# One head of a score pair: read from PSUM by ScalarE in place of a VectorE copy in SBUF

## The chip, the core and the metric

The kernel runs on one core of a Trainium2 chip. Its engines work side by side, each through its own list of instructions in order: TensorE (PE in the profile; its weight loads are listed as PEld) multiplies matrices and writes into PSUM, VectorE (DVE) and ScalarE (ACT) do elementwise work, GpSimd (POOL) some more of it, and SyncE (SP) issues DMAs. Engines wait for each other through semaphores. The metric is the device time of one execution in microseconds; the time before is the median of three runs.

## The reference

Two attention layers over 2048 positions with 32 heads of 18 dimensions, model width 576; their outputs stand side by side in `out`. Layer A is multi-query: 32 query heads share one key head and one value head, and every position attends to every other.

```
q = (x @ wq) as 32 heads;  k = x @ wk;  v = x @ wv          # A: one k, one v
p = softmax(q @ k^T * 18**-0.5);  out_A = concat(p @ v) @ wo
```

Layer B cuts the sequence into four segments of 512. In a segment each head does causal attention, and adds what a running memory of the earlier segments gives (a linear attention with its own denominator), weighed by a gate per head:

```
a_dot = softmax(q_s @ k_s^T * scale + mask) @ v_s
a_mem = phi(q_s) @ M / (phi(q_s) @ z + 1e-6)
o = g * a_mem + (1 - g) * a_dot;   M += phi(k_s)^T @ v_s;  z += sum phi(k_s)
```

Almost all of the elementwise work is the exponential of layer A's scores: 32 heads x 2048 x 2048.

## The kernel before

A first part (up to about 288 us of the span) projects x to queries, keys and values and stores them in DRAM. Then comes the attention, where the change lies, and at the end (from about 1363 us) the last output projections.

The attention works in **items**. For layer A an item is 128 keys (`kt`, 16 of them) by 512 queries (chunk `c`, 4) for a group of four heads (`hg`, 8); it is done as two **pairs** of heads (`pr` 0 and 1). So 32 blocks (`c`, `hg`) have 32 pairs each. Blocks of layer B (3 items each) are strewn between the first ones. Pairs are taken three to a **turn**: `turns[k]` lists them, and since 32 isn't a multiple of three, the last turn of a block has two. A block of layer A thus has eleven turns.

The loop over turns (L1177 to L1217) gives the engines their order, which is kept for TensorE, ScalarE and VectorE (`manual_schedule`). In turn `k` it does:

- `scores` (L935) for each of the turn's pairs: two matmuls (one a head, L950) into a PSUM tile `E` of 128 x 2 x 512, which takes two of the eight PSUM banks. There are three E buffers (`psE`, `bufs=3`); the other two banks are `O` and `F`. A tile's buffer can be used again when all that reads the tile is done.
- the exponentials, one ScalarE activation a pair over both heads (L968), in the order first, third, second pair (L1180).
- `run_fill`: a part of an output projection or of the memory's read-out (tile `F`, L801, L857).
- one third of the pending VectorE exponential, `slow` (L1192).
- `products` (L981): the matmuls of P with the values into `O` (L998), for the items of two turns before.
- `due`: stores, loads and weighing steps whose turn has come. Weighing (L785) runs on GpSimd, and each step is ordered behind `gate[-1]`, the last VectorE instruction noted. While `slow` holds work, `due` hands out no weighing step.

The **second pair** of each turn is `copied`: VectorE copies it from E into an SBUF tile `W` (L965), and ScalarE reads W. That lets go of E without waiting for ScalarE, which comes to this pair last.

In some turns of layer A (`BY_DVE`, L56: item 0 and item 9 for the second pair of heads, item 5 for the first, the third of these only in blocks in `third`) VectorE makes the exponential of one of the two heads itself. The positions are such that this is always the turn's second pair. There are 86 such turns: 10 blocks with two and 22 with three. `exponentials` (L920) reads E's first head with one `tensor_scalar` (L924) in the turn itself, and six more VectorE instructions (L926 to L931) follow in the second, third and fourth turn after. The other head's scores are copied to W (the half copy, 128 x 512, L965) and ScalarE makes their exponential (`hs = slice(1, 2)`) into the same tile PD.

Of the kernel before, what the change touches and what calls it, by code (L numbers as in the profile page):

```python
# [14 lines left out]
ALU = mybir.AluOpType  # L15
# [35 lines left out]
EXP_A = LOG2 * 2.0 ** 23  # L51
EXP_B = (127.0 + math.log2(0.00011720523372930181)) * 2.0 ** 23
# [23 lines left out]
def attention_pair_kernel(ctx, tc, a_xT, a_w, a_wo, b_xT, b_w, b_wo, b_beta, ident_d, hmask_d, bmask_d, cmask_d, sel_d, zmask_d, selx_d, sely_d, out):  # L76
    nc = tc.nc
# [79 lines left out]
    with ExitStack() as ph:  # L157
# [256 lines left out]
        for s in range(NSEG):  # L414
# [110 lines left out]
            if not last:  # L525
                e = p2.tile([128, 4, DH], F32, name="ph31")
# [101 lines left out]
    with tc.If(loose > 0, preferred_fallthrough_block=False):  # L628
        with ExitStack() as ph:
# [37 lines left out]
            with tc.For_i(0, H, 1) as h:  # L667
# [5 lines left out]
                for i in range(NKT):  # L673
                    s, j = divmod(i, 4)
                    n = 128 * (j + 1)
# [241 lines left out]
    slow, now, gate, third = [], [0], [], set()  # L917
    AFTER = mybir.DependencyInfo(mybir.DependencyClass.Sync, mybir.DependencyReason.SCHED_ONLY)

    def exponentials(p, e, whole):  # L920

        u, w = (pp.tile([128, 512], F32, name=nm, bufs=1) for nm in "nq")
        v, stt, y = nc.vector, nc.vector.scalar_tensor_tensor, p.bitcast(U32)
        v.tensor_scalar(y, e, EXP_A, EXP_B, op0=ALU.mult, op1=ALU.add)  # L924
        ops = [
            lambda: v.tensor_scalar(u.bitcast(U32), y, MANTISSA, ONE_BITS, op0=ALU.bitwise_and, op1=ALU.bitwise_or),  # L926
            lambda: v.tensor_scalar(w.bitcast(U32), y, EXPONENT, None, op0=ALU.bitwise_and),
            lambda: stt(p, u, POLY[0], u, op0=ALU.add, op1=ALU.mult),  # L928
            lambda: stt(p, p, POLY[1], u, op0=ALU.add, op1=ALU.mult),
            lambda: stt(p, p, POLY[2], p, op0=ALU.add, op1=ALU.mult),  # L930
            lambda: stt(p, p, POLY[3], w, op0=ALU.add, op1=ALU.mult),  # L931
        ]
        slow.extend((now[0] + 2 + i, p, ops[2 * i : 2 * i + 2], whole) for i in range(3))

    def scores(it, pr, copied):  # L935

        ab, c, hg, kt = it
        st = stacks[ab, c, hg // 2]
        h = 2 * (hg % 2) + pr
        e = psE.tile([128, 2, 512], F32, name="E")  # L940
        if ab == "A" and (kt, pr) == THIRD and not any(cost and k <= now[0] + 4 for k, cost, *_ in later):
            third.add((c, hg))
        dve = ab == "A" and (kt, pr) in by_dve(c, hg)
        p = pp.tile([128, 2, 512], F32, name="PD" if dve else "P", bufs=2 if dve else PBUFS)
        state[it, pr] = p
        n = 512 if ab == "A" else 512 - 128 * kt if kt < 2 else 384
        if ab == "A":
            for j, r0 in enumerate(HALF):
                rows = slice(r0, r0 + KR)
                nc.tensor.matmul(e[:, j], kstA[rows, 128 * kt : 128 * kt + 128], st[rows, h, :], start=True, stop=True)  # L950
            if dve:
                exponentials(p[:, 0], e[:, 0], p)
        else:
            for k, c0 in BKEYS[kt]:
                ks = slice(128 * k, 128 * k + 128)
                for j, r0 in enumerate(HALF):
                    rows = slice(r0, r0 + KR)
                    nc.tensor.matmul(  # L958
                        e[:, j, c0 : c0 + 512 - 128 * k], st[rows, 4 + h, ks], st[rows, h, 128 * k :], start=True, stop=True
                    )  # L960
        src, hs = e, slice(0, 2)
        if copied:
            src = pp.tile([128, 2, 512], F32, name="W", bufs=2)
            hs = slice(1, 2) if dve else slice(0, 2)
            gate.append(nc.vector.tensor_copy(src[:, hs, :n], e[:, hs, :n]))  # L965

        def exponential():
            nc.scalar.activation(p[:, hs, :n], src[:, hs, :n], AF.Exp, scale=SCALE)  # L968
            if ab == "B":

                m = len(BKEYS[kt])
                diag = p.rearrange("p a (b t) -> p a b t", t=256)[:, :, 0:m, 0:128]
                nc.gpsimd.affine_select(  # L973
                    diag, diag, pattern=[[0, 2], [0, m], [1, 128]], base=0, channel_multiplier=-1, compare_op=ALU.is_ge, fill=0.0
                )

        return exponential
# [36 lines left out]
    def by_dve(c, hg):  # L1014

        return [x for n, x in enumerate(BY_DVE) if n < 2 or (c, hg) in third]
# [112 lines left out]
    with tc.manual_schedule(engines={ENG.PE, ENG.Activation, ENG.DVE}):  # L1129
# [47 lines left out]
        for k in range(len(turns) + 2):  # L1177
            now[0] = k
            exps = [scores(its[n], pr, i == 1) for i, (n, pr) in enumerate(turns[k])] if k < len(turns) else []
            for i in (0, 2, 1) if len(exps) == 3 else range(len(exps)):  # L1180
                exps[i]()
# [167 lines left out]
```

## Time and profile before

| | |
|---|---|
| time, median of 3 runs | 1409.04 us (1406.99 to 1409.36) |
| span of the profiled execution, first to last instruction | 1404.7 us |
| TensorE matmuls busy | 1383.6 us, 98% |
| ScalarE busy | 1199.5 us, 85% |
| VectorE busy | 1047.3 us, 75% |
| GpSimd busy | 233.3 us, 17% |
| mean granted TensorE clock | 0.997 |

The page gives the profiled execution no time of its own beside the span; the span lies 4.3 us below the median of the runs. In the views a row has the start in us, the duration, the engine, the line, the operation, out<-in, shapes and a count; several instructions in a row of the same kind are merged into one row. Activations overlap: the next begins before the one ahead has written its last result, so that what an activation costs ScalarE is the distance from its start to the next start, and what a reader waits for is its end. Ends of matmuls are modelled. An idle time in brackets is followed by what ended it.

### The profile page before, as it was taken

What the parts mean: (1) busy time and instruction counts of PE and PEld (TensorE: products, weight loads), DVE (VectorE), ACT (ScalarE), POOL (GpSimd) and SP (SyncE); (2) the same over time, 40 slices, a digit from 0 to 9 for tenths busy, and PEclk for the clock granted to TensorE, in tenths of its full rate; (3) what the DMA queues carried; (4) which work ended last, traced back from release to release, by engine and by line L of the source; (5) the groups of instructions that cost most, each with busy time, mean ns of one, the idle gap of its engine ahead of it and who ended that gap; (6) DMA issues with size and microseconds to landing.
All of it is one profiled execution on the core that took longest, in us unless ns stands there. A gap on an engine that the chain in (4) does not pass through costs nothing.

```text
span 1404.7 us, 41217 instructions
## 1 busy us (share of the span) xinstructions
PE 1383.6 (98%) x17452; PEld 837.7 (60%) x17452; DVE 1047.3 (75%) x1563; ACT 1199.5 (85%) x1481; POOL 233.3 (17%) x335
## 2 busy tenths in 40 slices
PE   9999999989999999999999999999999999999998
PEld 6787888745554555555555555555555555555558
DVE  6656456467787778787878878777879778887884
ACT  4543434479999999999999999999999999999991
POOL 2441000003302310412110122113010220001002
PEclk9999999999999999999999999999999999999999
DMA  9766546567575345332322452233103321120023
GB/s 283 259 213 188 168 147 216 183 175 219 151 200 180 120 139 181 95 120 85 112 59 71 133 158 60 94 104 93 51 27 94 115 75 40 31 72 21 17 68 124
DMA packets 91284, 173.63 MB, mean 124 GB/s; under 512 B 14702, under 2 KB 23015, under 8 KB 90668
## 3 DMA queue, kind: packets, MB, share of 16 engines
q1 hardware_dynamic: 84680, 160.93, 36.9%
q0 software_dynamic: 1664, 4.78, 1.3%
q10 hardware_dynamic: 4752, 5.24, 1.2%
q8 instruction: 138, 2.26, 0.7%
q14 instruction: 50, 0.41, 0.1%
HBM read 99.65 MB, written 70.67 MB: 121 GB/s over the span
## 4 chain that ended last, share of the span: by engine, by line
PE 64%; ACT 6%; DVE 4%; issue 2%; DMA 1%; POOL 0%; SPq 0%; POOLq 0%; DVEq 0%; ACTq 0%
PE O L998 31%; PE E L950 19%; PE F L801 11%; ACT P L968 6%; PE E L958 3%; DVE W L965 2%; PE F L857 1%; DMA o<-oA 0%; DVE sm L750 0%; DVE PD L930 0%; DVE PD L928 0%; POOL o L785 0%; DMA rb<-rA 0%; DMA o<-o 0%; DVE o L862 0%
## 5 line engine op out<-in xcount | busy, mean ns | idle before, releaser
L968 ACT ACTIVATE P<-E 128x1024 f32<-128x1024 f32 (+1 forms) x800 | 787.6, 1076 | 4.4 <-PE E L950 4.2
L965 DVE COPY W<-E 128x1024 f32<-128x1024 f32 (+2 forms) x416 | 453.3, 1090 | 145.2 <-PE E L950 83.9
L998 PE MATMUL O<-P,VA 128*32 128x256 f32 x7504 | 507.6, 380 | 0.0
L968 ACT ACTIVATE P<-W 128x1024 f32<-128x1024 f32 (+1 forms) x330 | 369.9, 1121 | 6.1 <-DVE W L965 5.6
L998 PEld LDWEIGHTS O<-P,VA 128*32 128x32 f32 x7504 | 259.8, 110 | 138.0 <-issue 6.1
L950 PE MATMUL E<-stA,kstA 56*128 56x512 f32 x1920 | 317.0, 430 | 2.0 <-ACT P L968 1.8
L950 PEld LDWEIGHTS E<-stA,kstA 56*128 56x128 f32 x1920 | 155.3, 184 | 158.3 <-issue 94.2
L973 POOL TENSOR_SCALAR_AFFINE_SELECT P<-P 128x256 f32<-128x256 f32 (+1 forms) x192 | 94.6, 493 | 414.7 <-ACT P L968 376.7
L785 POOL TENSOR_TENSOR o<-o,rb 126x512 f32<-126x512 f32 (+1 forms) x55 | 72.8, 1348 | 431.1 <-DVE PD L931 185.1
L801 PE MATMUL F<-woB,o 126*32 126x192 f32 (+1 forms) x1920 | 126.6, 338 | 0.0
L998 PE MATMUL O<-PD,VA 128*32 128x256 f32 x688 | 88.9, 379 | 0.0
L801 PEld LDWEIGHTS F<-woB,o 126*32 126x32 f32 (+1 forms) x1920 | 38.7, 108 | 74.9 <-issue 69.6
L998 PE MATMUL O<-P,vseg 128*32 128x256 f32 (+2 forms) x1536 | 81.4, 344 | 0.1
L924 DVE TENSOR_SCALAR PD<-E 128x512 uint32<-128x512 f32 x86 | 59.2, 689 | 23.5 <-PE E L950 21.7
L1007 DVE COPY oe<-O 128x512 f32<-128x512 f32 x64 | 44.3, 692 | 42.4 <-PE O L998 39.8
L253 PE MATMUL pj<-xh,wBh 128*126 128x512 f32 x180 | 72.2, 401 | 0.0
L253 PE MATMUL pj<-xh,wBl 128*126 128x512 f32 x180 | 71.7, 398 | 0.0
L122 ACT CAST qp<-pj 126x512 fp32r<-126x512 f32 (+1 forms) x54 | 31.0, 584 | 44.2 <-DVE kmB L459 27.8
L123 DVE TENSOR_TENSOR qp<-pj,qp 126x512 fp32r<-126x512 f32 (+1 forms) x54 | 36.8, 686 | 37.8 <-ACT qp L122 37.8
L801 PE MATMUL F<-woA,o 126*32 126x192 f32 (+1 forms) x960 | 64.0, 338 | 0.0
L958 PE MATMUL E<-stB 56*128 56x256 f32 (+3 forms) x512 | 61.6, 348 | 2.1 <-ACT P L968 1.3
L998 PEld LDWEIGHTS O<-P,vseg 128*32 128x32 f32 x1536 | 49.0, 110 | 24.3 <-issue 1.9
(206 smaller groups left out, 1573.2 us busy)
## 6 DMA issues: line engine op xcount, KB each, us to landing
stB<-kB SPq DMA_DIRECT2D x96, 144.0 KB
stB<-qB SPq DMA_DIRECT2D x32, 288.0 KB
stA<-qA SPq DMA_DIRECT2D x30, 288.0 KB
oA<-oe SPq DMA_DIRECT2D x32, 256.0 KB
oB<-oe SPq DMA_DIRECT2D x32, 256.0 KB
qA<-qp SPq DMA_DIRECT2D x16, 504.0 KB
kB<-qp SPq DMA_DIRECT2D x16, 504.0 KB
qB<-qp SPq DMA_DIRECT2D x16, 504.0 KB
```

The lines of the kernel that those rows point to most:

```text
L123: hold(nc.vector.tensor_tensor(qp[:R, 1, :n], src, qp[:R, 0, :n].bitcast(F32), op=ALU.subtract))
L253: nc.tensor.matmul(dst, w[:, c0 : c0 + M], x, start=i == 0, stop=i == len(ops) - 1)
L785: ins = tc.keep_in_program_order(nc.gpsimd.tensor_tensor(dst, a, b, op=op))
L801: nc.tensor.matmul(dst[32 * j : 32 * j + 32], parts[ab, c][: RT[t], t, r0 : r0 + 32], wo[ab][: RT[t], t, c0 : c0 + n], start=start, stop=stop,
L924: v.tensor_scalar(y, e, EXP_A, EXP_B, op0=ALU.mult, op1=ALU.add)
L950: nc.tensor.matmul(e[:, j], kstA[rows, 128 * kt : 128 * kt + 128], st[rows, h, :], start=True, stop=True)
L958: nc.tensor.matmul(e[:, j, c0 : c0 + 512 - 128 * k], st[rows, 4 + h, ks], st[rows, h, 128 * k :], start=True, stop=True)
L965: gate.append(nc.vector.tensor_copy(src[:, hs, :n], e[:, hs, :n]))
L968: nc.scalar.activation(p[:, hs, :n], src[:, hs, :n], AF.Exp, scale=SCALE)
L973: nc.gpsimd.affine_select(diag, diag, pattern=[[0, 2], [0, m], [1, 128]], base=0, channel_multiplier=-1, compare_op=ALU.is_ge, fill=0.0)
L998: nc.tensor.matmul(o[32 * j : 32 * j + 32, q0 : q0 + n], v, p[:, j % 2, p0 : p0 + n], start=m == hf == 0, stop=last and hf == 1,)
L1007: nc.vector.tensor_copy(osb, o)
```

## The change

In `scores`, a pair of which VectorE makes one head is not copied any more: `src` stays E and only the other head (`slice(1, 2)`) goes through the activation, out of PSUM. The other second pairs are copied as before. So that the list `gate` still has an entry for such a turn, the `tensor_scalar` at the head of `exponentials` is put into it.

```diff
@@ def exponentials
-        v.tensor_scalar(y, e, EXP_A, EXP_B, op0=ALU.mult, op1=ALU.add)
+        gate.append(v.tensor_scalar(y, e, EXP_A, EXP_B, op0=ALU.mult, op1=ALU.add))
@@ def scores
-        src, hs = e, slice(0, 2)
-        if copied:
+        src, hs = e, slice(1, 2) if dve else slice(0, 2)
+        if copied and not dve:
             src = pp.tile([128, 2, 512], F32, name="W", bufs=2)
-            hs = slice(1, 2) if dve else slice(0, 2)
-            gate.append(nc.vector.tensor_copy(src[:, hs, :n], e[:, hs, :n]))
+            gate.append(nc.vector.tensor_copy(src[..., :n], e[..., :n]))
```

## The prediction

> **What bounds the kernel now.** I read the page's busy times first, then the busy times of the attention part alone, then the waits, then the order of time inside one block. The views agree that two engines are full at once.
>
> ```profile
> PE 1383.6 (98%) x17452; PEld 837.7 (60%) x17452; DVE 1047.3 (75%) x1563; ACT 1199.5 (85%) x1481; POOL 233.3 (17%) x335
> ...
> 288.00:1362.00 1074.00, 1066.72 (x15244) 576.17 (x15248) 862.97 (x1204) 1064.30 (x1215) 177.07 (x261) 1.00 0.33 101
> ...
> ACT P L968 <- DVE W L965: 5.6, 13, 0.8
> ACT P L968 <- PE E L950: 4.2, 5, 2.0
> ACT PD L968 <- DVE W L965: 0.5, 1, 0.5
> ...
> by line: PE O L998 47.5%; PE E L950 34.7%; PE F L801 18.4%
> ```
>
> The second line is the stretch from 288 to 1362 us: TensorE is busy 1066.7 of 1074 us and ScalarE 1064.3; the columns after them show VectorE at 863 and GpSimd at 177. ScalarE waits 10.3 us in all. The last line is the chain of waits over 1160 to 1185 us: there it never leaves TensorE. So the stage is paced by TensorE and ScalarE in turn, with about 10 us of room on either; VectorE has 20% free.
>
> How one turn runs is seen in a block of eleven turns late in the kernel, of which the first, fourth and seventh are changed turns (those with a half activation PD). First ScalarE, from the half activation of the first changed turn on, then TensorE's six score matmuls of the turns behind:
>
> ```profile
> 1165.36 0.63 ACT L968 ACTIVATE PD<-W 128x512 f32<-128x512 f32 x1
> 1165.89 1.94 ACT L968 ACTIVATE P<-E 128x1024 f32<-128x1024 f32 x2
> 1167.69 1.08 ACT L968 ACTIVATE P<-W 128x1024 f32<-128x1024 f32 x1
> 1168.64 1.96 ACT L968 ACTIVATE P<-E 128x1024 f32<-128x1024 f32 x2
> ...
> 1171.40 1.97 ACT L968 ACTIVATE P<-E 128x1024 f32<-128x1024 f32 x2
> 1173.20 0.69 ACT L968 ACTIVATE PD<-W 128x512 f32<-128x512 f32 x1
> 1173.72 1.99 ACT L968 ACTIVATE P<-E 128x1024 f32<-128x1024 f32 x2
> ...
> 1181.04 0.74 ACT L968 ACTIVATE PD<-W 128x512 f32<-128x512 f32 x1
> 1181.63 1.97 ACT L968 ACTIVATE P<-E 128x1024 f32<-128x1024 f32 x2
> ...
> 1184.40 1.06 ACT L968 ACTIVATE P<-E 128x1024 f32<-128x1024 f32 x1
> ```
>
> ```profile
> 1165.14 0.96 PE L950 MATMUL E<-stA,kstA 56*128 56x512 f32 x6
> 1167.79 0.96 PE L950 MATMUL E<-stA,kstA 56*128 56x512 f32 x6
> 1170.43 0.97 PE L950 MATMUL E<-stA,kstA 56*128 56x512 f32 x6
> 1173.10 0.95 PE L950 MATMUL E<-stA,kstA 56*128 56x512 f32 x6
> ...
> 1181.03 0.96 PE L950 MATMUL E<-stA,kstA 56*128 56x512 f32 x6
> 1183.68 0.96 PE L950 MATMUL E<-stA,kstA 56*128 56x512 f32 x6
> ```
>
> TensorE needs 2.65 us a turn (1167.79 to 1170.43). ScalarE needs 2.75 in a plain turn (1165.89 to 1168.64: two activations of 0.90 and one out of W of 0.95) and 2.32 in a changed one (1171.40 to 1173.72: the PD activation holds it 0.52 only). Three turns with one changed cost ScalarE 7.82 and TensorE 7.95: a tie, which is why a wait moved onto either is hardly covered.
>
> **The change part by part.**
>
> ```profile
> L965 DVE COPY W<-E 128x512 f32<-128x512 f32 x86 | 58.5, 681 | 0.0
> L968 ACT ACTIVATE PD<-W 128x512 f32<-128x512 f32 x86 | 61.6, 716 | 0.5 <-DVE W L965 0.5
> ```
>
> *Removed: 86 copies of half a pair.* VectorE loses 58.5 us of its 863. It is not on the path; what can be won is ScalarE's waits for a copy, 5.6 + 0.5 us, and only those that fall within a turn or two of a changed turn, since a copy removed shortens VectorE's queue by about 0.6 us there and nowhere else. Bounds: 0 and 6.1. I take 1.5.
>
> *Moved: the operand of 86 activations from SBUF to PSUM.* No row has a 128x512 activation out of E. The nearest are the full ones: from one start to the next, 0.90 out of E (1171.40 to 1173.20 is two) and 0.95 out of W (1167.69 to 1168.64). If the difference is per instruction, the half one falls from 0.52 to 0.475: 86 x 0.045 = 3.9 us of ScalarE time; if it is per element, half that; if the half form shows none, 0. I take 0.045, and carry it in the walk below.
>
> *Added: E is kept longer.* There are three E buffers for three pairs a turn. The copy gave the second pair's buffer back early; ScalarE takes the pairs in the order first, third, second, so now that buffer comes free with the last activation of the turn. What TensorE does when a copy is late is shown by one turn of before:
>
> ```profile
> 527.39 2.01 ACT L968 ACTIVATE P<-E 128x1024 f32<-128x1024 f32 x2
> 528.10 0.67 DVE L965 COPY W<-E 128x512 f32<-128x512 f32 x1
> 529.09 0.19 PEld L950 LDWEIGHTS E<-stA,kstA 56*128 56x128 f32 x2 [0.41 <-issue]
> 529.09 1.11 PE L950 MATMUL E<-stA,kstA 56*128 56x512 f32 x6
> 529.46 0.30 PEld L950 LDWEIGHTS E<-stA,kstA 56*128 56x128 f32 x4 [0.18 <-ACT P L968]
> ...
> L950 PE MATMUL E<-stA,kstA x1920: 382/393/503, 384.2 to 1360.7; 56*128 56x512 f32 x192
> ```
>
> The copy had ended at 528.77, yet the second pair (529.46) waited for ScalarE's second activation (end 529.40): the buffers are handed on in the order in which they were expected free. I therefore let the next turn's second pair take the third pair's buffer, and its *third* pair the one now kept by the PD activation. Also from these rows: 0.06 us from the end of an activation to the weight load, and a scores row of 1.11 instead of 0.96 for a pair that started 0.03 late, so a stalled pair costs 0.11 more to refill the pipeline. The third pair is due 0.57 after the first (0.96 less the median 0.39). Queued behind the waiting matmul are the turn's F and O matmuls and the next turn's scores; ScalarE waits for those. How soon it does:
>
> ```profile
> 475.52 0.95 PE L950 MATMUL E<-stA,kstA 56*128 56x512 f32 x6
> 476.06 1.94 ACT L968 ACTIVATE P<-E 128x1024 f32<-128x1024 f32 x2
> ```
>
> This is a turn in which ScalarE stood ready; an activation begins 0.54 after its pair's first matmul.
>
> Now the walk through the block. *First changed turn.* The PD activation ends at 1165.36 + 0.63 - 0.04 = 1165.95; the third pair may start at 1166.01 instead of 1165.14 + 0.57 = 1165.71: 0.30 + 0.11 = **0.41 us late**, and everything on TensorE behind it. The next scores start at 1167.79 + 0.41 = 1168.20, ScalarE can begin at 1168.74, but is ready at 1168.64 - 0.05 = 1168.59: it is now 0.10 behind the old trace. *Second.* PD starts at 1173.30 and ends at 1173.95; the third pair, due at 1173.10 + 0.41 + 0.57 = 1174.08, no longer waits (1174.01). But ScalarE, ready at 1173.30 + 0.475 = 1173.78, waits for the scores begun at 1173.51: until 1174.05, now 0.33 behind. *Third.* PD from 1181.37 to 1182.07; the third pair, due at 1182.01, starts at 1182.13: 0.12 + 0.11, TensorE 0.64 behind. ScalarE starts the next turn at 1181.44 + 0.54 = 1181.98 (0.35 behind) and the one after at 1183.68 + 0.64 + 0.54 = 1184.86 (0.46 behind).
>
> So such a block loses 0.46 us by ScalarE's count and 0.64 by TensorE's, and the plain turns that follow, at 2.65 and 2.75, give neither back. I take 0.50 for three changed turns, 0.167 each: 86 x 0.167 = 14.4 us, with the 0.045 already in it. Less the 1.5 of copy waits, **about +13 us**; I add 1 for blocks where the half activation is longer than here (its mean is 0.716, in this block 0.63 to 0.74): **+14**.
>
> *Moved: the entry in `gate`* from the copy to the tensor_scalar ahead of it. GpSimd's weighing is not handed out while the list `slow` holds work, and it does from the changed turn on, so the entry used is a later one: 0. Without that cover a GpSimd step would start 0.6 us earlier, with GpSimd 17% busy. No DMA is issued, removed or moved past another on SP's or GpSimd's queue. The W tile is taken 86 times less; only copies wait for it.
>
> **The rivals.**
>
> *A, TensorE has room and takes the wait in.* Then only the savings stay: 3.9 us of activations and up to 6.1 of copy waits, -4 to -10, say 1403. It decides at 0.4 us of slack a changed turn. For it: ScalarE is as full as TensorE, and where the turn holds less TensorE work the stall is free. Against it: the turn is 2.65 with or without a wait, and the chain between 1160 and 1185 is TensorE alone. The Trainium skill speaks for A: its page "Perfetto Trace Analysis", section "Identifying the Most-Contended Engine", says that matmul busy time is no good measure of how full TensorE is and that the weight loads' share should be used. By that rule the 576 of 1074 us of weight loads would leave nearly half free, and the result would be A's; I hold the chain against it, since the matmuls of a turn follow each other without a gap.
>
> *B, stall and savings cancel.* The first pair of turns loses 0.10 only; if the refill of 0.11 isn't paid and VectorE's shorter queue ends most copy waits, the sum is within 2.8 us of zero: 1409.
>
> *C, the buffers are handed on in the fixed order*, so that the next turn's second pair waits for the last activation. It is due some 0.28 earlier than the third, so each changed turn loses about 0.2 us more: +14 + 17 = +31, 1440. Against it: the row at 529.46.
>
> That the change doesn't do what it says would show as PD<-W rows; I give it nothing, the edit being two lines.
>
> **How the numbers follow.** The profiled execution's span is 1404.7 us; +14 makes 1418.7. The median of the runs, 1409.04, is 4.3 above the span, so I predict 1409 + 14 = 1423 us. Chances: forecast 0.58 (its own range 1413 to 1432), C 0.12, B 0.16, A 0.14. The range that holds 8 in 10 reaches from the upper part of A to C: 1404 to 1440. A measurement of this kernel can tell 0.2% (2.8 us) from no change: faster 0.14, same 0.16, slower 0.70.
>
> **What the changed profile would show.** 86 rows PD<-E in place of PD<-W, near 0.68 us each, held 0.475 from start to start; 330 copies in place of 416. In the turn after a changed one, score weight loads that wait for ScalarE's PD activation, for the third pair (if for the second, C holds). ScalarE's waits for TensorE's scores, now 4.2 us, grow to 15 or more: that is the loss itself. If they stay under 6 us, A or B is right. Waits of ScalarE on W near 6 us mean that nothing was won on VectorE. The forecast is wrong if a changed turn is followed by scores on time, or if TensorE's turn shrinks below 2.65.

## The result and the profile after

| | before | after |
|---|---|---|
| time, median (lowest to highest of the runs taken together) | 1409.2 us (1406.99 to 1409.36) | 1421.44 us (1420.54 to 1422.1) |
| span of the profiled execution | 1404.7 us | 1418.4 us |
| mean granted TensorE clock | 0.997 | 0.995 |

The changed kernel takes 1.0093 times as long, with an interval of 1.0078 to 1.0107: 12.2 us more by the medians, 13.7 by the spans. The granted clock differs by 0.002, which would be worth 3 us at the most (0.002 of 1409, an estimate), so at least three quarters of the time were lost in the order of the work.

The busy times of the page after, and the busy times of the attention alone (engine by engine in the order PE, PEld, DVE, ACT, POOL):

```profile
PE 1397.3 (99%) x17452; PEld 837.9 (59%) x17452; DVE 1002.7 (71%) x1477; ACT 1205.1 (85%) x1481; POOL 234.2 (17%) x335
...
288.00:1376.00 1088.00, 1080.61 (x15250) 577.23 (x15251) 818.43 (x1118) 1070.41 (x1215) 177.60 (x261) 1.00 0.33 100
```

VectorE has 44.6 us less to do over the span and 86 instructions fewer. From the first score matmul to the last turn of the attention it is 14.4 us more than before, so all of the loss lies there (the stretch shown is 14 us longer than the one of before, 288 to 1362), and TensorE counts as busy in nearly all of it again. That share can't show the stall, since the rows of a stalled turn (below) have it inside the busy time of the score matmuls. The waits show it.

What TensorE's weight loads wait for, in the attention part of before and then of after (us in total, times, longest). A weight load is the first instruction of a score matmul, so it carries the wait for a free E:

```profile
PEld E L950 <- issue: 99.8, 245, 1.9
PEld E L950 <- ACT P L968: 59.3, 159, 1.1
```

```profile
PEld E L950 <- ACT P L967: 101.4, 259, 1.4
PEld E L950 <- issue: 52.3, 131, 1.4
PEld E L950 <- ACT PD L967: 22.8, 81, 0.7
```

The last row is new: 81 of the 86 half activations are now what a score load waited for, and each of these 81 loads is that of a third pair. The other two rows say less than they seem to. Most of both is the bracket that every turn's first load has anyway, 0.41 us whether it is put down to issue or to ScalarE (1174.54 below, and 0.41 again at 1177.62, there under ScalarE's name); between the traces it has mostly changed its name.

The operations of the changed lines after (columns: busy us, mean ns of one, idle ahead of it):

```profile
L967 ACT ACTIVATE P<-E 128x1024 f32<-128x1024 f32 x704 | 694.8, 1047 | 10.9 <-PE E L950 5.4
L964 DVE COPY W<-E 128x1024 f32<-128x1024 f32 x298 | 364.5, 1223 | 164.8 <-PE E L950 128.9 <-ACT P L967 24.0 <-PE E L958 8.5
...
L967 ACT ACTIVATE PD<-E 128x512 f32<-128x512 f32 x86 | 54.3, 631 | 0.3 <-DVE PD L924 0.3
...
L964 DVE COPY W<-E 128x768 f32<-128x768 f32 x32 | 30.6, 958 | 32.9 <-PE E L958 31.0 <-ACT P L967 1.9
```

All 86 half activations read E, and 298 + 32 = 330 copies are left: the change does what it says.

Now the block of turns at the place of the one in the prediction, first on ScalarE, then TensorE's matmuls with the score weight loads of the middle turn (start, duration):

```profile
1174.77 0.60 ACT L967 ACTIVATE PD<-E 128x512 f32<-128x512 f32 x1
1175.25 1.95 ACT L967 ACTIVATE P<-E 128x1024 f32<-128x1024 f32 x2
1177.06 1.09 ACT L967 ACTIVATE P<-W 128x1024 f32<-128x1024 f32 x1
1178.22 1.94 ACT L967 ACTIVATE P<-E 128x1024 f32<-128x1024 f32 x2
```

```profile
1172.32 0.96 PE L950 MATMUL E<-stA,kstA 56*128 56x512 f32 x6
...
1174.54 1.39 PE L950 MATMUL E<-stA,kstA 56*128 56x512 f32 x6
1175.86 0.53 PE L801 MATMUL F<-woA,o 126*32 126x192 f32 x8
...
1177.62 0.96 PE L950 MATMUL E<-stA,kstA 56*128 56x512 f32 x6
1178.51 0.53 PE L801 MATMUL F<-woA,o 126*32 126x192 f32 x8
```

```profile
1174.54 0.19 PEld L950 LDWEIGHTS E<-stA,kstA 56*128 56x128 f32 x2 [0.41 <-issue]
1174.93 0.19 PEld L950 LDWEIGHTS E<-stA,kstA 56*128 56x128 f32 x2 [0.21 <-ACT P L967]
1175.42 0.19 PEld L950 LDWEIGHTS E<-stA,kstA 56*128 56x128 f32 x2 [0.30 <-ACT PD L967]
```

The half activation runs from 1174.77 to 1175.37, and 0.05 us later the third pair's weights are loaded, at 0.88 after the turn's first matmul. In a turn without a wait all six follow each other (the row at 1172.32: 0.96 for the six). The scores take 1.39 instead of 0.96, the F matmuls begin at 1.32 instead of 0.89, and the next scores come 3.08 us after this turn's (1177.62 less 1174.54) where the turn took 2.65 before. ScalarE begins the third of its activations at 1177.06, could begin the next at 1177.06 + 0.95 = 1178.01, and begins it at 1178.22, 0.60 after the scores.

Over all 32 blocks, in the turn after a changed one, by the place of the changed turn in its block (from the starts of the score matmuls in the two traces, all 86 turns; means for the third pair's start after the turn's first matmul, medians for the turn's length; the last column counts the turns that are over 0.2 us longer than the same turn of before):

| changed turn of the block | third pair, before | after | turn's length, before | after | over 0.2 us longer |
|---|---|---|---|---|---|
| first | 0.64 us | 0.91 us | 2.65 us | 3.08 us | 22 of 32 |
| second | 0.59 | 0.67 | 2.65 | 2.73 | 10 of 32 |
| third | 0.59 | 0.62 | 2.65 | 2.77 | 1 of 22 |

These are 33 long turns in 32 blocks: one in each of 31 blocks, two in one. A block has one stall, mostly behind its first changed turn. In nine of the ten blocks where the first is spared, all of which follow a block of layer B, its half activation has ended about 0.5 us after the next turn's first matmul, before the third pair is due at 0.57; there the second has the stall. Behind a stall ScalarE runs less far behind TensorE: in the second changed turn its first activation began 0.99 us after the turn's first score matmul before and 0.73 after (medians), and its half activation ended 0.87 us after the next turn's first matmul before and 0.49 after. So the third pair then finds its buffer nearly free when it is due.

### The profile page after: what moved, and what is told of

It reads as the page before. It is cut to its first block, busy times and chain, and to the rows that moved or that the text cites. A ratio compares the mean times of both kernels' runs of the same rounds, so it can differ in the third digit from the quotient of the medians.

```text
span 1418.4 us, 41046 instructions
## 1 busy us (share of the span) xinstructions
PE 1397.3 (99%) x17452; PEld 837.9 (59%) x17452; DVE 1002.7 (71%) x1477; ACT 1205.1 (85%) x1481; POOL 234.2 (17%) x335
## 3 DMA queue, kind: packets, MB, share of 16 engines
q1 hardware_dynamic: 84680, 160.93, 36.4%
## 4 chain that ended last, share of the span: by engine, by line
PE 70%; ACT 4%; DVE 3%; issue 2%; DMA 1%; SPq 0%; POOLq 0%; DVEq 0%; ACTq 0%
PE O L997 33%; PE E L950 21%; PE F L801 11%; ACT P L967 4%; PE E L958 3%; DVE W L964 1%; PE F L857 1%; DVE P L1142 1%; DMA rb<-rA 0%; DMA o<-o 0%; DVE sm L750 0%; DVE PD L928 0%; DVE PD L930 0%; DVE P L1161 0%; SPq L812 0%
## 5 line engine op out<-in xcount | busy, mean ns | idle before, releaser
L967 ACT ACTIVATE P<-E 128x1024 f32<-128x1024 f32 (+1 forms) x800 | 767.2, 1025 | 10.9 <-PE E L950 5.4
L964 DVE COPY W<-E 128x1024 f32<-128x1024 f32 (+1 forms) x330 | 395.1, 1197 | 197.7 <-PE E L950 128.9
L967 ACT ACTIVATE P<-W 128x1024 f32<-128x1024 f32 (+1 forms) x330 | 353.7, 1072 | 8.5 <-DVE W L964 8.4
L950 PE MATMUL E<-stA,kstA 56*128 56x512 f32 x1920 | 330.5, 438 | 2.8 <-ACT P L967 2.3
```

Source lines behind the costliest of these rows:

```text
L964: gate.append(nc.vector.tensor_copy(src[..., :n], e[..., :n]))
```

## The experiments

For each, the ratio is that to the kernel before, on the same chip. Differences in us are ratios times 1407.

**The entry in `gate` alone.** The kernel before, with only the one line of `exponentials` changed.

```diff
-        v.tensor_scalar(y, e, EXP_A, EXP_B, op0=ALU.mult, op1=ALU.add)
+        gate.append(v.tensor_scalar(y, e, EXP_A, EXP_B, op0=ALU.mult, op1=ALU.add))
```

> The kernel before, with nothing of the change but the entry in `gate` for the tensor_scalar of a changed turn (the half copy is made and noted as well). My theory (the cost is the E buffer kept until ScalarE has read it): no difference, 1409 within 3 us. Rival (the order given to GpSimd's weighing steps takes part in the loss): slower, up to the changed kernel's 1421.

Measured: 1406.63 us, ratio 1.0002 (0.9992 to 1.0011). This part of the change costs nothing, as the prediction priced it.

**The late release without VectorE's relief.** The changed kernel, in which VectorE still makes the 86 half copies, into a W that nobody reads.

```diff
             gate.append(nc.vector.tensor_copy(src[..., :n], e[..., :n]))
+        elif copied:
+            spare = pp.tile([128, 2, 512], F32, name="W", bufs=2)
+            nc.vector.tensor_copy(spare[:, hs, :n], e[:, hs, :n])
```

> The changed kernel, but VectorE makes the 86 half copies all the same, into a W tile that nobody reads; ScalarE reads E. The buffer is kept as long as in the changed kernel, VectorE has its old load. Theory: the changed kernel's time or a little over it, 1421 to 1425, since VectorE's relief was worth 1.5 us. Rival (VectorE's relief is worth much and hides a larger loss): over 1427. Rival (the time went into something that the missing copy changes on VectorE, not into the buffer): back to 1409.

Measured: 1422.52 us, 1.0115 (1.0098 to 1.0132). VectorE's work is that of before here, and only who frees E, and from where ScalarE reads, has changed; the loss is there in full. So it comes from that and not from what VectorE does next. The 44.6 us that VectorE gains are worth 3 us by the ratios (1.0115 against 1.0093) and 1 by the medians, and the intervals overlap: little, and not told from nothing.

**Only the first, or only the second changed turn of each block.** The changed kernel, with the half copy kept in all but the 32 turns of item 0 (in the other run of item 5, `(5, 0)` in the condition). The `tensor_scalar` is not put into `gate` in these two runs.

```diff
-        if copied and not dve:
+        if copied and not (dve and (kt, pr) == (0, 1)):
...
-            gate.append(nc.vector.tensor_copy(src[..., :n], e[..., :n]))
+            gate.append(nc.vector.tensor_copy(src[:, hs, :n], e[:, hs, :n]))
```

> The change in the first changed turn of each block alone (32 of the 86); the others copy as before. Theory (what counts is how late ScalarE runs behind TensorE, and a stall leaves less for the next): one such turn a block costs nearly as much as all three, 0.3 us a block: 1417 to 1420. Rival (each changed turn costs the same 12.2/86 = 0.14 us): 1409 + 4.5 = 1413.7.

> The change in the second changed turn of each block alone (32 of the 86). Theory: there ScalarE runs 0.9 to 1.1 us behind TensorE instead of 0.65, so that the third pair is late by itself although the walk of the prediction gave this turn no stall after a stalled first one: 0.3 us a block, 1418 to 1421. Rival (additive): 1413.7. First and second alone together then cost more than the whole change.

Measured: 1415.67 us, 1.0061 (1.0045 to 1.0078), and 1415.09 us, 1.0059 (1.0042 to 1.0076). Their waits on the half activation, first the run with the first turns, then that with the second:

```profile
PEld E L950 <- ACT PD L967: 9.0, 32, 0.3
```

```profile
PEld E L950 <- ACT PD L967: 9.3, 31, 0.3
```

In nearly each of the 32 turns the load of TensorE's third pair waits, 0.28 us in the mean (9.0 over 32), and a turn costs 0.27 us in the end (0.0061 x 1407 = 8.6 over 32); the turn behind the changed one takes 3.08 and 3.07 us in the median, the turns behind the untouched half copies 2.65. A changed turn thus costs about twice as much alone as in company, where it is 12.2 over 86 = 0.14. The two together would make 17 us, more than the whole change with its 22 further turns, though the intervals are too wide to settle this by the times. The traces settle it: behind the second changed turn the next turn grows by 0.16 us in the mean in the changed kernel, with a long turn in 10 of 32 blocks, and by 0.38 with 30 of 32 where it is changed alone; ScalarE is then 0.99 us behind in that turn, as in the kernel before, and not 0.73. So it is not the place in the block that decides: the first to stall spares the next one. Both runs came out a little below what was expected (1417 to 1421): in the walk one stall of 0.41 us was to cost 0.3 to 0.4.

**No second pair copied at all.** The changed kernel, with every second pair read out of E by ScalarE.

```diff
-            exps = [scores(its[n], pr, i == 1) for i, (n, pr) in enumerate(turns[k])] if k < len(turns) else []
+            exps = [scores(its[n], pr, False) for i, (n, pr) in enumerate(turns[k])] if k < len(turns) else []
```

> No second pair is copied at all: ScalarE reads E in every turn, and VectorE loses all 416 copies (the changed kernel drops 86). Theory: in every plain turn of layer A the next turn's third pair waits for the last activation, which ends 0.54 + 1.81 + 1.05 + 0.06 = 3.46 us after the turn's first score matmul, against 3.22 when it is due; with 0.11 for the refill a turn takes 3.0 us instead of 2.65 to 2.75: 1470 to 1520. Rival (ScalarE alone sets the pace): 330 x 0.045 = 15 us less, 1394.

Measured: 1468.81 us, 1.0437 (1.0415 to 1.0459), 61 us slower than before, a shade below the range. Its page's busy times, and what ScalarE and TensorE's loads wait for from 288 to 1376 us (its attention goes on to about 1423):

```profile
PE 1424.7 (97%) x17452; PEld 838.1 (57%) x17452; DVE 625.0 (43%) x1147; ACT 1209.8 (83%) x1481; POOL 231.7 (16%) x335
```

```profile
ACT P L967 <- PE E L950: 36.8, 85, 2.1
ACT P L967 <- PE E L958: 13.1, 26, 0.7
```

```profile
PEld E L950 <- ACT P L967: 191.3, 471, 1.3
```

VectorE is relieved of 420 us, and ScalarE's own work falls, since every activation out of E is 0.045 us shorter than one out of W; yet the kernel is slower by 4.4%. ScalarE now waits visibly for scores, 50 us against 4.2, and the loads wait 191 us for ScalarE against 59. What the copies buy is the early release of E, and the change gives that up in 86 of 416 places.

**Less work on TensorE.** Rival A says that with room on TensorE the stall is free. Both kernels, with four fifths of the matmuls of the output projections left out (only the first of the five input tiles is multiplied).

```diff
     def out_part(ab, c, i, t, dst, c0, n, start, stop):
+        if t:
+            return
...
-                stop=stop,
+                stop=True,
```

> The kernel before with four fifths of the output projections inside the attention left out (only the first of five input tiles is multiplied, so the output is not the reference's); TensorE has some 0.45 us less to do in four turns of five. It is the base for the run beside it. ScalarE then sets the pace alone: 1385 to 1402.

> The changed kernel with the same four fifths left out. Theory: with room on TensorE the stall of 0.4 us a changed turn is taken in, and only ScalarE's saving of 86 x 0.045 = 3.9 us stays: 2 to 5 us below the light version of before. Rival (the longer hold costs time whatever TensorE has to do): about 12 us above it.

Measured: 1402.08 us, 0.9962 (0.9947 to 0.9976), for the kernel before cut in this way, and 1403.25 us, 0.9968 (0.9955 to 0.998), for the changed one. The 12 to 14 us between the two kernels shrink to 1, which is within the intervals. Busy times in the stretch from 288 to 1362 us, cut kernel before, then cut kernel after:

```profile
288.00:1362.00 1074.00, 1036.36 (x13056) 515.75 (x13056) 860.28 (x1207) 1065.21 (x1221) 177.39 (x261) 1.00 0.33 101
```

```profile
288.00:1362.00 1074.00, 1035.66 (x13025) 516.23 (x13029) 814.71 (x1119) 1063.20 (x1217) 177.03 (x261) 1.00 0.33 101
```

And one changed turn of the cut kernel after, ScalarE and then TensorE (its lines are numbered two higher):

```profile
1164.47 0.69 ACT L969 ACTIVATE PD<-E 128x512 f32<-128x512 f32 x1
1164.95 2.04 ACT L969 ACTIVATE P<-E 128x1024 f32<-128x1024 f32 x2
1166.76 1.18 ACT L969 ACTIVATE P<-W 128x1024 f32<-128x1024 f32 x1
1167.71 2.06 ACT L969 ACTIVATE P<-E 128x1024 f32<-128x1024 f32 x2
```

```profile
1163.93 0.49 PE L952 MATMUL E<-stA,kstA 56*128 56x512 f32 x2
1164.73 0.98 PE L952 MATMUL E<-stA,kstA 56*128 56x512 f32 x4 [0.30 <-ACT P L969]
1167.08 0.96 PE L952 MATMUL E<-stA,kstA 56*128 56x512 f32 x6
```

TensorE waits here too, and longer, for ScalarE: the scores of the turn behind it are stretched from 0.96 to 1.78 us (1163.93 to 1165.71). But there is less work behind them, the next scores begin at 1167.08, 0.63 before ScalarE takes them (0.60 is what it needs), and ScalarE goes from 1164.47 to 1167.71 without a pause: 0.48, 1.81 and 0.95 us from start to start. It is not the stall that costs time but a stall in front of a full TensorE. The expected gain of 2 to 5 us for the changed kernel did not come: ScalarE's shorter half activation saves 3.9 us, and its waits grew by 3.7 (20.0 us against 16.3, by the sum over starts explained further below).

**ScalarE's order in the changed turns.** The changed kernel; in a changed turn ScalarE takes the pairs in the order first, second, third.

```diff
-            for i in (0, 2, 1) if len(exps) == 3 else range(len(exps)):
+            half = k < len(turns) and any(its[n][0] == "A" and (its[n][3], pr) in by_dve(*its[n][1:3]) for n, pr in turns[k])
+            for i in (0, 2, 1) if len(exps) == 3 and not half else range(len(exps)):
```

> The changed kernel, but in the 86 changed turns ScalarE takes the pairs in the order first, second (the half one), third. The second pair's buffer is free 0.9 us earlier, but the third's then comes last: its activation starts 1.38 after the first and ends at 2.43, against 2.44 for the half one in the old order. Theory (the last of three reads sets it): no difference to the changed kernel, 1418 to 1424. Rival (it is this one buffer): most of the loss is gone, 1409 to 1413.

Measured: 1422.7 us, 1.011 (1.0093 to 1.0127), the same as the changed kernel. Without a copy three pairs wait for ScalarE, and the last of them frees its buffer at the same time whichever it is.

**Work put in front of the third pair.** The changed kernel; in the turn after a changed one the F matmuls (a part of an output projection) go ahead of the third pair's scores, so that TensorE has work while the buffer is not free. The edit reaches 56 turns and not all 86: where F is not an output projection it does nothing, and for the third changed turn of a block `half` is worked out before `scores` has entered the block into `third`.

```diff
+            half_before, half = half, k < len(turns) and any(its[n][0] == "A" and (its[n][3], pr) in by_dve(*its[n][1:3]) for n, pr in turns[k])
...
+            for i, (n, pr) in enumerate(turns[k]) if k < len(turns) else []:
+                if i == 2 and half_before and memory is None:
+                    run_fill()
+                    mid = True
+                exps.append(scores(its[n], pr, i == 1))
...
```

> The changed kernel, but in the turn after a changed one TensorE multiplies that turn's part of an output projection (F) before the third pair's scores instead of after them; nothing else. The third pair is then due 1.1 us after the turn's first score matmul instead of 0.57, about when the half activation has ended, so TensorE has other work in the wait. Theory: TensorE's loss goes; ScalarE, 0.6 to 0.76 behind in such a turn, needs the third pair at 1.5 to 1.66 and gets it at 1.62, so that it loses up to 0.1 us each time and keeps its saving of 3.9 us: 1405 to 1412. Rival (the loss comes with reading PSUM itself, or with the missing copies): it stays at 1418 to 1424.

Measured: 1429.68 us, 1.0155 (1.014 to 1.0169). I had expected 1405 to 1412, the loss given back; it is worse by 8 us instead. One such turn:

```profile
1181.79 0.90 PE L950 MATMUL E<-stA,kstA 56*128 56x512 f32 x4
1182.04 0.60 ACT L967 ACTIVATE PD<-E 128x512 f32<-128x512 f32 x1
1182.20 0.19 PEld L950 LDWEIGHTS E<-stA,kstA 56*128 56x128 f32 x2 [0.22 <-ACT P L967]
...
1182.62 0.53 PE L801 MATMUL F<-woA,o 126*32 126x192 f32 x8
...
1183.09 0.19 PEld L950 LDWEIGHTS E<-stA,kstA 56*128 56x128 f32 x2 [0.30 <-issue]
1183.09 0.49 PE L950 MATMUL E<-stA,kstA 56*128 56x512 f32 x2
...
1183.51 0.84 PE L997 MATMUL O<-P,VA 128*32 128x256 f32 x10
...
1184.94 0.50 PE L950 MATMUL E<-stA,kstA 56*128 56x512 f32 x2
```

The third pair no longer waits for ScalarE: the half activation had ended at 1182.64, and the bracket at 1183.09 says issue. The wait is gone and the turn is longer, 3.15 us (1184.94 less 1181.79). The undivided order is that of the rows at 1177.62 and 1178.51 above: the second pair starts 0.34 after the first (the median of all turns), F at 0.89, and O, by the same trace, at 1178.86, which is 1.24. So from the second pair's start to O's it takes 0.90 us. Here it takes 1.31 (1182.20, from the two pairs' weight loads, to 1183.51), 0.41 more for the same matmuls, of which none waits for another engine. The other 0.07 is a wait of the second pair, which begins at 0.41 instead of 0.34. Going over from score matmuls to those of F and back once more costs about as much as the stall that it was to fill (0.43 with its refill), and it is paid where there was no stall too. Over all blocks the turn behind the first changed one takes 3.16 us in the median, where the changed kernel takes 3.08, and the one behind the second 3.00 against 2.73; that is most of the 8 us. So this run does not tell what the stall alone costs. A bracket on TensorE that ends in "issue" is not room.

**Fewer copies elsewhere.** The kernel before, in which the second pair of the last turn of a block (which has two) is read out of E; there the next turn has a buffer to spare.

```diff
-            exps = [scores(its[n], pr, i == 1) for i, (n, pr) in enumerate(turns[k])] if k < len(turns) else []
+            exps = [scores(its[n], pr, i == 1 and len(turns[k]) == 3) for i, (n, pr) in enumerate(turns[k])] if k < len(turns) else []
```

> The kernel before, its 86 half copies kept, but in the turns of two pairs the second pair is not copied: ScalarE reads E. There TensorE's next third pair is due 2.41 + 0.57 = 2.98 after the turn's first score matmul and the second activation has ended by 2.94 even with ScalarE 0.94 behind, so the longer hold should cost nothing; ScalarE saves 0.045 us in each of some 32 turns and no longer waits there for the copy (0.2 to 0.3 us in many blocks of the trace). Theory (the hold costs only where TensorE needs the buffer sooner): 1403 to 1408, that is faster by up to 4 us. Rival (any second pair read from PSUM costs): slower by 3 us or more.

Measured: 1408.91 us, 1.001 (1.0001 to 1.0019): no gain, where I had hoped for up to 4 us, but 1.4 us more, just clear of the noise. ScalarE's waits in the attention part:

```profile
ACT P L968 <- PE E L950: 4.0, 6, 2.2
ACT P L968 <- DVE W L965: 2.3, 6, 0.6
```

The waits for copies fell from 5.6 to 2.3 us as meant, but the time from one start to the next shows them again a few activations later, between the half activations of the next block and the ones behind them (8.1 us in all against 4.1, three quarters of the growth at the first changed turn). The activation that comes late there is the first of the next turn, which needs that turn's scores. No version was found that beats the kernel before.

## Why the prediction was right

**Time and range.** The forecast was 1423 us, +14; measured were 1421.44 and +12.2, with an interval of +11 to +15. Every one of the rivals lies outside of that interval.

**Where the loss arises.** The walk said that the next turn's third pair would wait for the half activation, by 0.30 us after the first changed turn, none after the second, and 0.12 after the third, with TensorE 0.41 us behind after the first and 0.64 in the end. In the 22 blocks that stall behind the first changed turn, as the one walked through, the next turn grows by 0.42 us in the median, those behind the second and third by 0.08 and 0.14: 0.64 in sum. The first stall is as walked. The third is smaller than the walked 0.23, and the 0.08 behind the second was not in the walk; that these two make up for each other is luck. The refill of 0.11, read from a single row of before, holds: the scores row grew from 0.96 to 1.39 for a pair that came 0.88 - 0.56 = 0.32 late. One block was walked through for all 32; that the other ten have their stall behind a later changed turn was not foreseen, and that it leaves the sum nearly the same is luck as well.

**What of it reaches the end.** Over all blocks the turns behind changed ones grow by 17.5 us, 0.55 a block. The other turns of the attention give 3.1 us back, 2.2 in layer A and 0.9 in layer B, so that 14.4 are left; the part ahead of the attention is 0.8 us shorter in the trace after, and the span grows by 13.7. The plain turns thus give back little, as predicted. By the time of the kernel a block lost 12.2 / 32 = 0.38 us, with 2.7 changed turns. The prediction took 0.50 for three, between ScalarE's count and TensorE's, which makes 0.45 for 2.7. Why 0.50 and not either count it did not argue, so how near the 14 came is luck in part.

**ScalarE's shorter half activation.** The 0.045 us were confirmed. From the start of a half activation to the next start, the shortest is 0.472 us in the changed kernel and a tenth are under 0.477; before, the shortest was 0.518. The Trainium skill ("Perfetto Trace Analysis", section "Optimizing Scalar/DVE Operations") puts the fixed part of a ScalarE instruction at some 93 ns on SBUF and 51 on PSUM, a difference of 42; the trace agrees with that, and that it is per instruction: 45 ns for the half activation as for the full one. The saving is had only when ScalarE then has something to do: the median distance became 0.667, which is the loss as ScalarE sees it.

**ScalarE's waits.** Here the marker failed as it was printed. ScalarE's rows after, in the attention part:

```profile
ACT P L967 <- DVE W L964: 8.1, 23, 0.8
ACT P L967 <- PE E L950: 5.4, 8, 2.0
ACT PD L967 <- DVE PD L924: 0.3, 1, 0.3
```

"15 or more" was said of the waits for TensorE's scores, and "under 6 means A or B"; the view has 5.4, and neither A nor B is right. The view counts idle time from the end of an activation. An activation's end lies some 0.13 to 0.15 us behind the point at which the next one may start (0.60 long, held 0.475; 1.05 in the mean, held 0.903), so a pause of 0.2 us shows as next to nothing, and small ones aren't listed. Counted from start to start the loss is there. Take for each kind of activation the distance to the next start when nothing is waited for (0.903 us for 128x1024 out of E, 0.948 out of W, 0.521 and 0.476 for the half ones, 0.690 and 0.735 for 128x768) and sum what goes beyond it, over the attention, without what is 0.02 us and less:

| | needed | lost in waits |
|---|---|---|
| before | 1051.8 us | 20.1 us |
| after | 1048.0 | 36.4 |
| no copies at all | 1033.2 | 94.8 |

ScalarE needs 3.9 us less and loses 16.3 more: net 12.4, and 14.2 with the smallest pauses. Needed and lost together make up ScalarE's whole stretch, so the net must come out near the measured 12.2 to 13.7; the table tells how the loss divides, not what caused it. The marker asked for the right number of the wrong view. The rows of before that the prediction built on had the same blind spot: the 10.3 us that it read as ScalarE's waits, and as its room, are 20.1 counted from start to start.

**VectorE's relief.** I took 1.5 us out of a bound of 0 to 6.1. ScalarE's waits for W rose from 5.6 to 8.1 us instead of falling, probably since scores that come late make copies late; no run shows this apart. The run that keeps the copies puts the relief between nothing and 3 us. The size is not settled beyond that, and the 1.5 has no support.

**The "+1"** for half activations longer than in the block shown has no support: their mean fell from 0.716 to 0.631, below the 0.68 forecast for it. Without it the sum is 13. It nearly cancels the 1.5, so the forecast is near the measured time by its walk and not by these two.

**The `gate` entry** at 0 was right, by a run of its own.

**The rivals.** *A* failed for this kernel, and its condition was confirmed in part: with output projections cut, the change costs 1 us in place of 12, but it gains nothing either. The rule of the Trainium skill behind it ("Perfetto Trace Analysis", section "Identifying the Most-Contended Engine") names the weight loads' share beside MFU, which was not worked out here; the share alone would have put the room of TensorE at nearly half, and it stayed at 577 of 1088 us. The trace doesn't agree with it as a measure of room here: a stall of 0.43 us in a turn appears as a turn longer by 0.43. *B* is out by the interval, and neither of its conditions held: the refill is paid, and ScalarE's waits for copies rose. *C* is refuted by the bracket at 1175.42 and the 80 others like it: it is the third pair that waits for the half activation; the second waits for the activation ahead of it, 0.40 instead of 0.34 after the first.

## What to carry to other kernels

A copy that looks like wasted work on an idle engine may be there to give back a buffer. Before taking it out, find who frees the buffer then, who waits for that, and whether that engine has room in that very turn; here about 0.3 us of late release once a block, in front of a TensorE with no room, outweighed 45 us of VectorE time and 3.9 us of ScalarE time. To see small waits of a pipelined engine, count from start to start, since a list of idle times hides what lies under the tail of the instruction before.

## What the runs showed of the hardware that was not expected

**An activation's length depends on how long ScalarE has run without a pause.** A pause of before, and behind it three half activations in one block in which ScalarE hardly waits, with the two full activations that stand behind each:

```profile
1189.91 1.10 ACT L968 ACTIVATE P<-E 128x1024 f32<-128x1024 f32 x1
1191.15 1.06 ACT L968 ACTIVATE P<-W 128x1024 f32<-128x1024 f32 x1
1192.11 1.92 ACT L968 ACTIVATE P<-E 128x1024 f32<-128x1024 f32 x2
1193.92 0.63 ACT L968 ACTIVATE PD<-W 128x512 f32<-128x512 f32 x1
1194.44 1.94 ACT L968 ACTIVATE P<-E 128x1024 f32<-128x1024 f32 x2
...
1201.76 0.69 ACT L968 ACTIVATE PD<-W 128x512 f32<-128x512 f32 x1
1202.27 1.99 ACT L968 ACTIVATE P<-E 128x1024 f32<-128x1024 f32 x2
...
1209.59 0.74 ACT L968 ACTIVATE PD<-W 128x512 f32<-128x512 f32 x1
1210.15 2.01 ACT L968 ACTIVATE P<-E 128x1024 f32<-128x1024 f32 x2
```

Behind the first row ScalarE pauses for 0.33 us (1.24 to the next start in place of 0.90), and a full activation out of E, 1.10 long there, is 1.02 long right after (1.92 for two, less 0.90). Then the start-to-start distances stay the same (0.52, 0.51 and, with a small wait, 0.56 behind the half ones, 0.90 between full ones) while the ends drift back, by 0.11 us in 16 us. Over the whole attention of before a full activation out of E lasts 1.02 us in the mean in the first 4 us behind a pause of over 0.1 us, and 1.2 when ScalarE has run for 32 us or more without one. In the changed kernel, with more pauses, the full activation out of E has a mean of 1047 ns, where before it was 1104. So a longer mean was a sign of an engine kept busy, not of a slower one. What the hardware does there is not shown by these runs.

**Going from one kind of matmul to another costs TensorE time.** In the run with F ahead of the third pair, the same matmuls took 0.41 us longer for being cut into score, F, score and O matmuls instead of score, F and O. A turn of the old order has three such changes; what each of them costs was not measured apart.
